# Fewer half swaps, larger loads of v and a two-part PSUM copy in the opening of a gated-attention and feed-forward kernel

## The chip, the cores and the metric

The kernel runs on one core of a Trainium2 chip. The metric is the device time of one execution in microseconds (us); the figure of a kernel is the median of its runs. The engines are PE (the matrix engine; its weight loads are shown apart as PEld), DVE (vector), ACT (scalar), POOL (GpSimd) and SP (which here only issues DMAs). POOL also issues DMAs, and an instruction that waits on POOL holds up everything behind it in POOL's queue.

## The reference

```python
# u, v: (8, 3072, 256)   z: (8, 3072, 64)   w1, w2: (256, 1024)   w_out: (1024, 256)
scores = (1.0 / S) * np.matmul(z, z.transpose(0, 2, 1))
attn = np.maximum(scores, 0.0) ** 2
x = (u * np.matmul(attn, v)).reshape(B * S, D)
out = np.maximum(x @ w1, x @ w2) @ w_out
```

Eight batches are independent of each other up to the last two lines, which work on all 24,576 rows alike.

## The kernel before, in words

**Tiling.** Each batch has 3,072 rows, cut into 24 tiles of 128. Four tiles make a group of 512 rows (six groups a batch), two groups make a couple (three couples a batch, 24 in all), and eight tiles of v, z or u are a "piece". A block `A[b, g, k]` is the squared, rectified score of query group `g` against key group `k`, kept in bf16. The scores are symmetric, so only the blocks with k >= g are computed (`score_pair`: two PE matmuls at L217 into PSUM, a Relu on ACT at L230 or on DVE at L228, a square on DVE at L238 or L236); the others are DMA transposes of them (`mirror`, L269, issued by SP).

**The feed-forward part** of a group (`ff`) multiplies with w1 - w2 (L447), rectifies on ACT (L454), and multiplies with w_out and the product of w2 and w_out (L470, L461); results leave by ACT copies (L482) and DMAs that POOL issues (L483). `second` runs it for both groups of the couple before, with DVE tasks of the next couple hooked between its steps.

**Attention, first batch.** The first four groups (`for i in range(PLAIN)`, L612) go one by one: the 128 keys of a tile are contracted in two halves of 64 rows that run side by side on PE, each half with its own two PSUM banks, matmuls at L285. During the first group z's transposes are made on PE (`zT_pe`, L122): PE turns n tiles into a PSUM tile, and one copy (L129) takes them to `zT`. It is called four times: tiles 0 to 3 and 4 to 11 are copied by DVE, tiles 12 to 19 and 20 to 23 by ACT.

**Attention, the plain couple.** Couple i = 2, groups 4 and 5 of the first batch, is the only one in `PLAIN_COUPLES`. Its four outputs D11, D12, D21, D22 (group, then half of the 256 columns of v) own one PSUM bank each. Every step issues two matmuls at L897: one contracts the upper 64 rows of a tile (half 0), the other the lower 64 rows (half 1), for two different outputs. For each "superblock" (1,024 keys; the order is 2, 1, 0) there are four runs of eight steps, so 32 steps, and 96 in all. `PLAIN_LANES` says which output each half works on in each run: half 0 takes D11, D12, D21, D22 and half 1 takes D21, D22, D11, D12.

**Bank swaps.** When an output moves from one half to the other, the first matmul of the new half must come after the last of the old one. `steps_of_couple` finds these places (`marks`, `waits`). One step after the marked matmul the kernel puts a no-op on POOL that waits for it (L878, `relays`), and the first matmul of the new half waits for that no-op. In POOL's queue the no-op stands in program order among the DMA issues.

**Loads of v.** `load_v` (L151) takes a piece or a part of it; `step = 2 if b else n` (L157) cuts it into DMAs of two tiles for every batch but the first. In the plain couple a plan issues v of batch 1 by six calls of four tiles, at steps 12, 20, 28, 36, 44 and 52, so twelve DMAs (L159). Every DMA that POOL issues gets one of eight semaphores in turn, and the built program lets an issue wait until the DMA eight issues before it has landed. DVE forms differences of v of batch 1 (`combine_v`, L173 to L176) in the feed-forward part after the plain couple.

**The other couples** (i >= 3) use seven products in place of eight and relay through ACT; nothing in them is edited.

## Time and profile before

| what | us |
|---|---|
| median of 6 runs | 911.57 |
| lowest and highest run | 909.49, 919.0 |
| the profiled execution, its own time | 911.91 |
| its span in the profile | 910.1 |
| PE busy | 898.8 (99%) |
| DVE, ACT, POOL busy | 723.0, 601.9, 163.8 |
| first group, up to the first drain | about 1 to 21 |
| plain couple, its matmuls | 80.06 to about 107.4 |
| v loads of batch 1 issued | 83.09 to 98.72 |
| DVE's differences of v of batch 1 | 114.14 to 119.3 |

The span is the stretch that the profile covers; 1.81 us of the execution lie outside it. A wait is listed with the engine and line that waited, an arrow, and what released it. "POOLq L878" is the no-op of a bank swap in POOL's queue. The engines' granted clock is full in every slice.

### The profile page before, as it was taken

What the parts mean: (1) busy time and instruction counts of PE and PEld (TensorE: products, weight loads), DVE (VectorE), ACT (ScalarE), POOL (GpSimd) and SP (SyncE); (2) the same over time, 40 slices, a digit from 0 to 9 for tenths busy, and PEclk for the clock granted to TensorE, in tenths of its full rate; (3) what the DMA queues carried; (4) which work ended last, traced back from release to release, by engine and by line L of the source; (5) the groups of instructions that cost most, each with busy time, mean ns of one, the idle gap of its engine ahead of it and who ended that gap; (6) DMA issues with size and microseconds to landing.
All of it is one profiled execution on the core that took longest, in us unless ns stands there. A gap on an engine that the chain in (4) does not pass through costs nothing.

```text
span 910.1 us, 19395 instructions
## 1 busy us (share of the span) xinstructions
PE 898.8 (99%) x7478; PEld 521.1 (57%) x7526; DVE 723.0 (79%) x1093; ACT 601.9 (66%) x1191; POOL 163.8 (18%) x309
## 2 busy tenths in 40 slices
PE   9999999999999999999999999999999999999998
PEld 4456455565565555665656656566465564655655
DVE  6773689879998799887997979979799788995640
ACT  7887866667676676667676666666766567673445
POOL 3103021212111121202113023030320212101000
PEclk9999999999999999999999999999999999999999
DMA  9999999999999996999989999899988999887201
GB/s 187 180 205 190 148 193 174 154 169 163 175 194 152 170 188 115 198 164 167 169 138 195 150 150 184 146 179 162 174 172 148 173 167 170 161 159 146 74 24 71
DMA packets 397421, 145.61 MB, mean 160 GB/s; under 512 B 362000, under 2 KB 389264, under 8 KB 397328
## 3 DMA queue, kind: packets, MB, share of 16 engines
q1 hardware_dynamic: 359040, 91.79, 65.3%
q0 software_dynamic: 38288, 52.58, 32.4%
q8 instruction: 59, 0.97, 0.5%
q14 instruction: 34, 0.28, 0.1%
HBM read 59.77 MB, written 25.17 MB: 93 GB/s over the span
## 4 chain that ended last, share of the span: by engine, by line
PE 95%; DMA 2%; DVE 1%; issue 1%; ACT 0%; POOL 0%; ACTq 0%; POOLq 0%
PE acc L897 44%; PE o_ps L470 18%; PE d_ps L447 18%; PE s_ps L217 7%; PE o_ps L461 5%; PE acc L285 3%; DMA v_sb<-in_v_dram 1%; DMA blk<-blk 1%; DVE blk L238 0%; PE acc L590 0%; ACT r_sb L230 0%; PE w2o_ps L679 0%; DVE w_sb L662 0%; ACT zT L129 0%; DVE blk L236 0%
## 5 line engine op out<-in xcount | busy, mean ns | idle before, releaser
L897 PE MATMUL acc<-blk,v_sb 64*128 64x512 bf16 x2208 | 451.0, 376 | 1.6 <-POOLq L878 1.6
L230 ACT ACTIVATE r_sb<-s_ps 128x512 bf16<-128x512 f32 (+3 forms) x672 | 335.9, 559 | 122.3 <-PE s_ps L217 79.9
L897 PE MATMUL acc<-blk,vt 64*128 64x512 bf16 x1512 | 364.4, 376 | 0.0
L897 PEld LDWEIGHTS <-v_sb 64*128 64x128 bf16 x2208 | 176.2, 94 | 135.0 <-issue 6.9
L238 DVE TENSOR_TENSOR blk<-r_sb 128x1024 bf16<-128x1024 bf16 x257 | 172.5, 689 | 89.6 <-ACT r_sb L230 89.0
L454 ACT ACTIVATE g_sb<-d_ps 128x512 bf16<-128x512 f32 x384 | 193.3, 630 | 28.6 <-PE acc L897 18.0
L470 PE MATMUL o_ps<-w_out_sb,g_sb 128*128 128x256 bf16 x1536 | 175.5, 273 | 0.0
L897 PEld LDWEIGHTS <-vt 64*128 64x128 bf16 x1512 | 139.2, 94 | 62.9
L447 PE MATMUL d_ps<-xT,w_sb 128*128 128x512 bf16 x720 | 167.7, 379 | 2.6 <-issue 0.2
L470 PEld LDWEIGHTS <-g_sb 128*128 128x128 bf16 x1536 | 150.3, 98 | 17.4
L482 ACT COPY o_sb<-o_ps 128x512 f32<-128x512 f32 (+1 forms) x98 | 56.3, 577 | 132.4 <-PE o_ps L470 132.4
L483 POOL DMA_DIRECT2D out_dram<-o_sb x88 | 48.1, 547 | 530.8 <-ACT o_sb L482 500.5
L774 DVE TENSOR_TENSOR h_sb<-h_sb,acc 128x512 f32<-128x512 f32 x168 | 109.4, 682 | 28.3 <-ACT h_sb L778 20.9
L217 PE MATMUL s_ps<-zT 64*128 64x512 bf16 (+3 forms) x676 | 126.3, 358 | 0.5 <-ACT zT L129 0.4
L447 PEld LDWEIGHTS <-w_sb 128*128 128x128 bf16 x768 | 73.3, 98 | 89.3 <-issue 9.7
L341 DVE TENSOR_TENSOR blk<-blk,blk 128x2048 bf16<-128x2048 bf16 x63 | 77.2, 1225 | 5.9 <-DMA blk<-blk 3.7
L337 DVE TENSOR_TENSOR blk<-blk,blk 128x2048 bf16<-128x2048 bf16 x63 | 76.8, 1219 | 0.0
L789 DVE TENSOR_TENSOR blk<-blk,blk 128x2048 bf16<-128x2048 bf16 x63 | 76.6, 1219 | 0.0
L345 DVE TENSOR_TENSOR blk<-blk,blk 128x2048 bf16<-128x2048 bf16 x63 | 73.3, 1219 | 1.8 <-DMA blk<-blk 1.7
L431 DVE SCALAR_TENSOR_TENSOR xT<-h_sb,uT 128x512 bf16<-128x512 f32 x96 | 62.0, 685 | 4.7 <-PE o_ps L461 4.7
L187 POOL DMA_DIRECT2D un<-in_u_dram x94 | 50.6, 564 | 80.0 <-DMA uT<-un 75.9
L236 DVE TENSOR_TENSOR blk<-r_sb 128x512 bf16<-128x512 bf16 (+3 forms) x162 | 46.5, 324 | 19.7 <-ACT r_sb L230 18.7
(48 smaller groups left out, 359.6 us busy)
## 6 DMA issues: line engine op xcount, KB each, us to landing
out_dram<-o_sb POOLq DMA_DIRECT2D x88, 256.0 KB, 3.6
un<-in_u_dram POOLq DMA_DIRECT2D x92, 128.0 KB, 5.4
v_sb<-in_v_dram POOLq DMA_DIRECT2D x86, 128.0 KB, 6.2
blk<-blk SPq DMA_TRANSPOSE x240, 4.9
zn<-in_z_dram POOLq DMA_DIRECT2D x21, 128.0 KB, 4.0
out_dram<-o_sb SPq DMA_DIRECT2D x6, 256.0 KB, 2.0
v_sb<-in_v_dram POOLq DMA_DIRECT2D x5, 256.0 KB, 7.7
blk<-in_moe_w_dram POOLq DMA_DIRECT2D x2, 512.0 KB, 7.1
```

The lines of the kernel that those rows point to most:

```text
L217: nc.tensor.matmul(s_ps[h][:, lo[h] :], zT[rows, z_at(b, blk * G + tiles[h]), :], zT[rows, q + lo[h] // P : q + G, :].rearrange("p t c -> ...
L230: nc.scalar.activation(o, s, AF.Relu)
L238: nc.vector.tensor_mul(a[:, k : k + 2, :], r, r)
L337: nc.vector.tensor_add(*alike(f["S1"], f["A21"], f["A22"]))
L341: nc.vector.tensor_sub(*alike(f["S2"], f["S1"], f["A11"]))
L345: nc.vector.tensor_sub(*alike(f["S3"], f["A11"], f["A21"]))
L447: nc.tensor.matmul(d_ps, w15_sb[:, kc, ts(nb, P)], xT[:, kc, :], start=(kc == 0), stop=(kc == KD - 1),)
L454: nc.scalar.activation(g_sb[:, nb, :], d_ps, AF.Relu)
L470: nc.tensor.matmul(o_ps[t // 2][:, t % 2, :], g_sb[:, nb, ts(t, P)], w_out_sb[:, nb, :], start=False, stop=(nb == KF - 1 and t % 2 == 1),)
L774: nc.vector.tensor_add(out, a, b_)
L789: nc.vector.tensor_sub(f["A12"].ap, f["A12"].ap, f["S2"].ap)
L897: mm = nc.tensor.matmul(a.out(acc[name]), w()[rows], a.moving(rows, j), start=name not in opened, stop=left[name] == 0,)
```

## The change

Three edits, none of which touches the arithmetic of a result other than the order of some additions.

- `zT_pe` copies its PSUM tile in parts of four tiles. The two calls with eight tiles (tiles 4 to 11 on DVE, 12 to 19 on ACT) now issue two copies each; the two calls with four tiles are as before.
- `load_v` takes the whole of what it is asked for in one DMA for batch 1 too, and the plan of the plain couple issues the six calls at steps 17, 25, 33, 41, 49 and 57. So six DMAs of four tiles stand where twelve of two tiles stood. Batches 2 and up keep two tiles a DMA.
- `plain_steps` reverses the lanes of every second superblock: in the second one half 0 takes D21, D22, D11, D12. An output then stays in its half from one superblock to the next, and only the swaps inside the superblocks are left: 12 in place of 20. No-ops stand after steps 7, 15, 39, 47, 71 and 79 (two each); before, they stood after every eighth step from 7 to 79.

```diff
         copy = nc.scalar.copy if engine == "act" else nc.vector.tensor_copy
-        copy(zT[:, lo : lo + n, :], tp)
+        for k in range(0, n, G):
+            copy(zT[:, lo + k : lo + k + G, :], tp[:, k : k + G, :])
...
-        step = 2 if b else n
+        step = 2 if b > 1 else n
...
-            for o in supers
-            for names in zip(*PLAIN_LANES)
+            for n, o in enumerate(supers)
+            for names in zip(*PLAIN_LANES[:: 1 - 2 * (n % 2)])
...
-                    *((12 + 8 * k, load_v, 1, k // 2, k % 2 * G, G) for k in range(6)),
+                    *((17 + 8 * k, load_v, 1, k // 2, k % 2 * G, G) for k in range(6)),
```

In the built program PE's instructions are the same in number and, but for the lanes, in order; DVE and ACT have one copy more each, POOL six DMA issues fewer. The first score matmul after a split copy waits for the copy's first part; a later one waits for the second.

## The prediction

> **What bounds the kernel now.** I read the page first, then who waited for whom on PE, then the timelines of the places where it waited.

> ```profile
> PE 898.8 (99%) x7478; PEld 521.1 (57%) x7526; DVE 723.0 (79%) x1093; ACT 601.9 (66%) x1191; POOL 163.8 (18%) x309
> ...
> DMA  9999999999999996999989999899988999887201
> ...
> L897 PE MATMUL acc<-blk,v_sb 64*128 64x512 bf16 x2208 | 451.0, 376 | 1.6 <-POOLq L878 1.6
> ```

> PE is busy for 898.8 of 910.1 us, so 11.3 us of idle time is all that reordering can win. The DMA engines are nearly full from start to end, but that costs only where PE waits for them. The third line is the one large group with idle time ahead of it: 1.6 us, ended by a no-op in POOL's queue (L878), a bank swap of the plain couple. The view of waits, PE alone (total, times, longest):

> ```profile
> PE acc L897 <- POOLq L878: 1.6, 1, 1.6
> ...
> PE s_ps L217 <- ACT zT L129: 0.4, 1, 0.4
> PE acc L285 <- DVE blk L238: 0.4, 1, 0.4
> PE acc L285 <- DMA blk<-blk: 0.3, 1, 0.3
> ```

> Two of these belong to what is edited: the swap, once, and the copy of z's turns by ACT, once. So 19 of 20 swaps cost PE nothing. By stretches, PE idles 0.78 us from 8 to 21, 0.93 to 43, 0.21 to 61, 0.11 to 80, 1.59 to 107 and 0.11 to 124: 3.73 us in all. From 124 to 852 it is 2.1 us of 728, so PE sets the pace there and a shift at 107 reaches the end undiminished.

> **The swap that stalls.** POOL's timeline in the plain couple (start, duration, idle time before and its releaser):

> ```profile
> 85.22 1.06 POOL L159 DMA_DIRECT2D v_sb<-in_v_dram  x2 [1.04 <-PE acc L897]
> ...
> 91.55 0.53 POOL L159 DMA_DIRECT2D v_sb<-in_v_dram  x1 [0.95 <-PE s_ps L217]
> 94.17 0.53 POOL L159 DMA_DIRECT2D v_sb<-in_v_dram  x1 [2.10 <-DMA v_sb<-in_v_dram]
> 96.04 0.53 POOL L159 DMA_DIRECT2D v_sb<-in_v_dram  x1 [1.34 <-DMA v_sb<-in_v_dram]
> 98.72 0.53 POOL L159 DMA_DIRECT2D v_sb<-in_v_dram  x1 [2.15 <-DMA v_sb<-in_v_dram]
> ```

> The last three issues wait for earlier v loads to land. They are the 10th to 12th of twelve, and each waits for the issue eight before it: the 12th for the 4th, issued at 85.75 (second of the pair at 85.22), which lands at 98.7, 13 us later. The no-op of the next swap stands behind it. PE at that time:

> ```profile
> 96.47 0.81 PE L897 MATMUL acc<-blk,v_sb 64*128 64x512 bf16 x6
> 98.87 0.60 PE L897 MATMUL acc<-blk,v_sb 64*128 64x512 bf16 x4 [1.59 <-POOLq L878]
> ```

> PE stops at 97.28 and resumes at 98.87. A step takes (27.33 - 1.59) / 96 = 0.268 us, so 97.28 is step (97.28 - 80.06) / 0.268 = 64, the border between the second superblock and the third.

> **The change part by part.**

> *Reversed lanes.* The swaps at steps 32, 40, 64 and 72 (two outputs' worth at each border) disappear, and with them the stalled one. Eight no-ops of 17 ns are nothing on POOL, which is 18% busy. Kept are the no-ops issued at steps 8, 16, 40, 48, 72 and 80, needed eight steps (2.1 us) later. The matmuls are as many as before, at the same places, and read the same blocks in the same steps, so no transposed block is needed sooner.

> *Six loads.* The loads at steps 17, 25, 33, 41, 49 and 57 start at about 80.06 + 0.268 s: 84.6, 86.8, 88.9, 91.0, 93.2 and 95.3. Eight issues back of each are the output DMAs at 71.47 and 73.22 and the four u loads from 73.76 to 75.4. Each lies 13 us or more before the load that waits for it, and the page gives 3.6 and 5.4 us as the median landing of the two kinds. So no load waits for a landing, and no no-op is held: those of step 40 precede their load, those of 48 stand behind one issue of 0.53 us, and those of 72 and 80 come 15 steps and more after the last load. Either edit alone should free step 64; together they save the 1.6 us once, not twice. POOL's six issues less (6 x 0.53 = 3.2 us) are hidden: POOL is idle there most of the time, and without that cover they would be a gain.

> *Landing.* DVE reads v of batch 1 only later:

> ```profile
> 114.14 0.42 DVE L173 TENSOR_TENSOR vt<-v_sb 128x512 bf16<-128x512 bf16 x1
> ...
> 117.58 0.42 DVE L173 TENSOR_TENSOR vt<-v_sb 128x512 bf16<-128x512 bf16 x1
> ```

> The third piece (last two loads) is read at 117.58, or 115.6 after a gain of 2 us: 20.3 us after its last issue at 95.3. DMA in the plain couple (count, KB each, median us to landing):

> ```profile
> v_sb<-in_v_dram POOLq DMA_DIRECT2D x12, 128.0 KB, 10.9
> ...
> blk<-blk SPq DMA_TRANSPOSE x2, 14.6
> ```

> A load of twice the bytes may take from 10.9 (if the queue of transposes sets it) to twice that, 21.8 (if its own bytes do). I take 13, near the first, because the bytes are as many as before and are asked for over a shorter time; then it lands at 108, with 7 us to spare. The transposes of this stage (longest landing 19.1 us, done by 108.4) are first read from 110.5 on.

> [...] I count nothing beyond the stall. [...]

> *The two-part copy.* The opening (several engines, one answer):

> ```profile
> 6.81 5.04 ACT L230 ACTIVATE r_sb<-s_ps 128x512 bf16<-128x512 f32 x9 [0.91 <-PE s_ps L217]
> 6.82 0.68 DVE L129 COPY zT<-tpz 128x1024 bf16<-128x1024 bf16 x1
> ...
> 11.38 1.04 PE L285 MATMUL acc<-blk,v_sb 64*128 64x512 bf16 x8
> 11.74 1.02 ACT L129 COPY zT<-tpz 128x1024 bf16<-128x1024 bf16 x1
> 12.81 0.39 PE L217 MATMUL s_ps<-zT 64*128 64x512 bf16 x2 [0.39 <-ACT zT L129]
> 13.24 0.60 ACT L230 ACTIVATE r_sb<-s_ps 128x512 bf16<-128x512 f32 x1 [0.48 <-PE s_ps L217]
> ```

> On ACT the first part takes 0.59 us (the four-tile copy at 16.36), so it ends at 11.74 + 0.59 = 12.33, and PE, free at 12.42, need not wait: 0.39 less. The second part ends near 12.9 instead of 12.76; the next ACT instruction waits for PE until 13.24, 12.87 after the shift, so at most some 0.03 comes back. I take 0.37. On DVE the first part (0.42) ends at 7.24 instead of 7.50, so the score at 7.55 can start about 0.26 sooner; but ACT works without a break from 6.81 to 11.8 on nine activations and then the copy, and it is the copy that PE awaits, so nothing is gained. DVE's extra 0.16 falls before an instruction that waits for ACT at 7.93.

> [...] Whether the 0.37 survives is less sure: at 20.93 and 37.9 PE waits again for DVE (0.4) and for a transpose (0.3). Their releasers follow PE's earlier work, so they should shift too, but with full DMA engines a landing may not. Bounds: 0 (nothing carried; the loss of 0.16 is hidden) to 0.39.

> *Sum*, on the profiled execution: 911.91 - 1.6 - 0.37 = 909.94 (span 908.1). It stands 0.34 above the median, so against the median 911.57 - 1.97 = 909.6.

> **Rivals.**

> 1. The opening's shift is swallowed by the waits at 20.9 or 37.9; only the swap is won: 911.57 - 1.6 = 910.0. For it: those waits exist, and DMA is full there. Against: they are released by work that follows PE.
> 2. The change does not do what it says: POOL is held by something else and PE stops at a kept swap (56, 80 or 88) for as long: 911.6. For it: loads still stand between swaps. Against: all eight-back landings are over.
> 3. More than the sum: fewer DMAs relieve the opening's and the plain couple's other waits. The cap is all of PE's idle time from 8 to 124, 3.73: 907.8.
> 4. Slower: the last load lands late behind SP's transposes and DVE's differences start late. DVE's last sum for the next couple ends at 127.48 and is wanted near 128.7 (step 20 of it), 1.2 us of slack. So a landing of more than 20.3 + 1.2 = 21.5 us costs PE one for one, and from 23.5 on the kernel is slower than before. At 26 us it is 911.57 - 1.97 + 4.5 = 914.1. For it: 19.1 us was seen in that stage for a transpose. Against: the loads' longest was 13.

> **How the numbers follow.** Chances: forecast 0.55, rivals in order 0.22, 0.05, 0.12, 0.06. The time is the forecast's, 909.6. The six runs spread from 909.49 to 911.91 with two above, so about 1 us of noise stands on each case: the forecast's own range is 908.5 to 911, and with rival 3 below and rivals 1 and 2 above 907.3 to 912.2. Over 1% (9.1 us), about what a measurement can tell from no change, lies beyond the cap of 3.73 for a gain (0.02, if the median's high runs fall away or appear) and needs a landing above 32 us for a loss (0.03). So 0.95 within 1%.

> **What the profile after would show.** Right: no wait of L897 for L878; no load L159 waiting for a v landing, all six issued by 96; no wait of L217 for L129; the plain couple 25.7 us long; a span near 908.1. Wrong: a wait for L878 at another step (rival 2), L173 waiting for a v landing and idle time of L897 after 123 (rival 4), or the waits at 20.9 and 37.9 grown by 0.4 (rival 1).

## The result and the profile after

| | median, us | lowest to highest |
|---|---|---|
| before, same chip | 916.23 (69 runs) | 909.44 to 924.45 |
| after | 915.0 (32 runs) | 909.48 to 924.17 |

The ratio is 0.9991 [0.9972, 1.0011]: no change that a measurement can tell. The forecast of "within 1%" holds. The time does not: 915.0 lies above the range of 907.3 to 912.2, and so does the kernel before, whose 69 runs have a median 4.7 us above that of the six that the forecast started from. Every ratio in this document leaves out the runs that are over 1.5% longer than the fastest of their kernel; below, this matters for e7, where 12 of 22 runs are left out, so that there the median tells more.

The profiled execution after took 913.1 us (span 911.3, mean granted clock 0.998). Its page, beside the first fence of the prediction (busy time, then groups by line; L897 is now L898, L217 is L218):

```profile
PE 898.8 (99%) x7478; PEld 519.9 (57%) x7526; DVE 724.4 (79%) x1094; ACT 602.0 (66%) x1192; POOL 160.9 (18%) x303
...
L898 PE MATMUL acc<-blk,v_sb 64*128 64x512 bf16 x2208 | 451.8, 378 | 0.0
...
L218 PE MATMUL s_ps<-zT 64*128 64x512 bf16 (+3 forms) x676 | 126.0, 358 | 2.2 <-DMA zT<-zd 2.0
```

The large group has lost its 1.6 us of idle time, as forecast. Another group has got 2.0 us: a score matmul that waited for a transpose of z. The view of waits, PE alone:

```profile
PE s_ps L218 <- DMA zT<-zd: 2.0, 1, 2.0
PE acc L286 <- DVE blk L239: 1.8, 2, 1.4
```

The wait for POOL's no-op and the wait for ACT's copy are gone from the list; the one for DVE's square has grown from 0.4 to 1.8. What the edits did can be seen in the timelines. POOL's loads of v:

```profile
85.02 1.62 POOL L160 DMA_DIRECT2D v_sb<-in_v_dram  x3 [3.61 <-PE acc L898]
95.47 0.53 POOL L160 DMA_DIRECT2D v_sb<-in_v_dram  x1 [8.84 <-PE s_ps L218]
97.33 1.06 POOL L160 DMA_DIRECT2D v_sb<-in_v_dram  x2 [1.33 <-PE s_ps L218]
```

All six wait for PE, none for a landing. They did not start at the times of their steps, though (forecast 84.6 to 95.3): three went out together from 85.02 on, and the other three at 95.47, 97.33 and 97.86, after a stop of PE that comes below. And the opening, ACT first, then PE:

```profile
12.41 1.08 ACT L130 COPY zT<-tpz 128x512 bf16<-128x512 bf16 x2
13.48 0.60 ACT L231 ACTIVATE r_sb<-s_ps 128x512 bf16<-128x512 f32 x1
```

```profile
11.91 1.04 PE L286 MATMUL acc<-blk,v_sb 64*128 64x512 bf16 x8
13.06 0.39 PE L218 MATMUL s_ps<-zT 64*128 64x512 bf16 x2
```

Two copies take 1.08 us (forecast 2 x 0.59 = 1.18) where one took 1.02, and PE's score starts 0.11 us after the matmuls ahead of it (11.91 + 1.04 = 12.95), not 0.39.

**Where the time went.** The n-th PE instruction of both traces can be laid side by side (7,478 in each). After minus before, in us, by the time in before: +0.67 at 10 (DVE's square of the opening held PE for 1.39 near 8 us; before that PE had been 0.64 ahead), +0.25 at 14 (0.42 won back, 0.27 of it at the copy), -0.22 at 39 (the wait for a mirror at 37.6 has fallen away), -0.23 at 86.5; then **+3.63** at 91; +1.87 at 99 (the no-op's wait is missing: -1.76); and +1.19 at the end (small differences over 800 us, -0.68). So between these two executions the forecast gains are there (1.76 and 0.27 for 1.6 and 0.37), and one new stop took 3.86 us. PE there:

```profile
86.32 0.81 PE L898 MATMUL acc<-blk,v_sb 64*128 64x512 bf16 x6
89.13 0.39 PE L218 MATMUL s_ps<-zT 64*128 64x512 bf16 x2 [2.00 <-DMA zT<-zd]
```

and by stretches of 1 us (length; busy time of PE, PEld, DVE, ACT and POOL; granted clock; DMA share, which counts a packet's whole time where it starts and so can pass 1; GB/s):

```profile
90.00:91.00 1.00, 1.00 (x8) 0.45 (x6) 0.33 (x1) 0.63 (x2) 0.00 (x0) 0.50 1.13 206
91.00:92.00 1.00, 1.00 (x8) 0.33 (x6) 0.36 (x1) 0.90 (x2) 0.00 (x0) 0.50 1.11 192
92.00:93.00 1.00, 1.00 (x8) 0.32 (x5) 0.69 (x1) 0.18 (x1) 0.00 (x0) 0.50 1.14 208
93.00:94.00 1.00, 1.00 (x10) 0.44 (x8) 0.00 (x0) 0.39 (x1) 0.00 (x0) 0.80 2.55 128
```

After the stop PE ran at half clock for 3.41 us (89.98 to 93.39). Of the 3.86, 2.00 are waiting and 1.70 slow matmuls (half of 3.41; the ledger grows from 1.93 to 3.63 over it), which "busy" does not tell from fast ones. The other 0.16 I put down to the overlap of neighbouring matmuls, which a stop breaks (at full clock a pair of scores is shown 0.38 long, the next matmul starting 0.22 after it began: 104.42 and 104.64 in after); likewise the no-op's wait of 1.59 is 1.76 in the ledger. The last section has what the traces show of the stops that half clock followed.

The wait is for z's second batch, which SP turns by DMA transposes. SP's queue in the kernel before, and after:

```profile
57.92 18.43 SPq L269 DMA_TRANSPOSE blk<-blk  x6
76.45 6.66 SPq L143 DMA_TRANSPOSE zT<-zd  x2
```

```profile
59.67 19.44 SPq L270 DMA_TRANSPOSE blk<-blk  x6
79.20 6.35 SPq L144 DMA_TRANSPOSE zT<-zd  x2
```

Before, PE's first use of a turn, and the time from issue to landing of the two turns:

```profile
87.19 0.38 PE L217 MATMUL s_ps<-zT 64*128 64x512 bf16 x2
DMA to landing us min/median/max: 9.8/10.2/10.6
```

The turns stand behind six mirrors and are issued one after another almost without a gap (76.35 to 76.45 in before, 79.11 to 79.20 in after). In the kernel before the first was issued at 76.45 and landed at 86.28, 0.9 us before PE used it at 87.19; after, it was issued at 79.20 and landed at 89.08. They took 9.8 and 9.9 us: after, it was late because it was issued late, and that because the mirrors ahead of it began 1.75 us later and took 1.0 longer. The slack was 0.9 us, which the forecast left out.

### The profile page after: what moved, and what is told of

Read it like the earlier page. It is cut to its first block, busy times and chain, and to the rows that moved or that the text cites. A ratio compares the mean times of both kernels' runs of the same rounds, so it can differ in the third digit from the quotient of the medians.

```text
span 911.3 us, 19380 instructions
## 1 busy us (share of the span) xinstructions
PE 898.8 (99%) x7478; PEld 519.9 (57%) x7526; DVE 724.4 (79%) x1094; ACT 602.0 (66%) x1192; POOL 160.9 (18%) x303
## 4 chain that ended last, share of the span: by engine, by line
PE 96%; DVE 1%; DMA 1%; issue 1%; ACT 1%; ACTq 0%; DVEq 0%
PE acc L898 44%; PE o_ps L471 18%; PE d_ps L448 18%; PE s_ps L218 7%; PE o_ps L462 5%; PE acc L286 3%; DMA zT<-zd 1%; DVE blk L239 1%; ACT r_sb L231 1%; PE acc L591 0%; PE w2o_ps L680 0%; DVE xT L432 0%; PE tpz L125 0%; DVE w_sb L663 0%; DVE h_sb L311 0%
## 5 line engine op out<-in xcount | busy, mean ns | idle before, releaser
L898 PE MATMUL acc<-blk,v_sb 64*128 64x512 bf16 x2208 | 451.8, 378 | 0.0
L898 PE MATMUL acc<-blk,vt 64*128 64x512 bf16 x1512 | 364.1, 376 | 0.0
L898 PEld LDWEIGHTS <-v_sb 64*128 64x128 bf16 x2208 | 176.6, 94 | 135.4 <-issue 7.8
L898 PEld LDWEIGHTS <-vt 64*128 64x128 bf16 x1512 | 139.2, 94 | 62.2
L775 DVE TENSOR_TENSOR h_sb<-h_sb,acc 128x512 f32<-128x512 f32 x168 | 109.5, 682 | 28.3 <-ACT h_sb L779 20.9
L218 PE MATMUL s_ps<-zT 64*128 64x512 bf16 (+3 forms) x676 | 126.0, 358 | 2.2 <-DMA zT<-zd 2.0
L188 POOL DMA_DIRECT2D un<-in_u_dram x94 | 50.8, 563 | 76.4 <-DMA uT<-un 71.2
L237 DVE TENSOR_TENSOR blk<-r_sb 128x512 bf16<-128x512 bf16 (+3 forms) x162 | 46.3, 323 | 19.9 <-ACT r_sb L231 18.9
## 6 DMA issues: line engine op xcount, KB each, us to landing
un<-in_u_dram POOLq DMA_DIRECT2D x92, 128.0 KB, 5.1
v_sb<-in_v_dram POOLq DMA_DIRECT2D x74, 128.0 KB, 5.4
zn<-in_z_dram POOLq DMA_DIRECT2D x21, 128.0 KB, 4.1
```

The source lines that it names most:

```text
L218: nc.tensor.matmul(s_ps[h][:, lo[h] :], zT[rows, z_at(b, blk * G + tiles[h]), :], zT[rows, q + lo[h] // P : q + G, :].rearrange("p t c -> ...
L775: nc.vector.tensor_add(out, a, b_)
L898: mm = nc.tensor.matmul(a.out(acc[name]), w()[rows], a.moving(rows, j), start=name not in opened, stop=left[name] == 0,)
```

## The experiments

All kernels compute the whole reference. The time of each (median, number of runs, ratio to the kernel before on the same chip with its interval), and PE's stops of 0.9 us or more after the opening, in its one profile:

| kernel | median (n) | ratio | stops of PE: at, us, for what | mean clock |
|---|---|---|---|---|
| e1 before | 915.89 (22) | 0.9981 [0.9954, 1.0008] | none | 0.999 |
| e2 lanes alone | 918.21 (14) | 1.0015 [0.9978, 1.0053] | 87.5, 8.23, z's turn | 0.996 |
| e3 loads alone | 915.01 (22) | 0.9984 [0.9957, 1.001] | 87.4, 3.06, z's turn | 0.998 |
| e4 copy alone | 915.09 (22) | 0.9976 [0.9948, 1.0003] | 36.8, 2.96, mirror | 0.998 |
| e5 after, z sooner | 915.84 (14) | 0.9986 [0.9955, 1.0017] | 37.2, 3.24, mirror; 180.1, 1.65, z's turn | 0.998 |
| e6 before, z sooner | 918.37 (22) | 0.9993 [0.9964, 1.0023] | 90.6, 8.57, mirror | 0.996 |
| e7 e5, w_out later | 925.66 (22) | 1.0025 [0.9986, 1.0064] | 37.4, 2.54, mirror; 92.0, 9.26, mirror | 0.994 |
| e8 after, u later | 914.72 (14) | 0.9998 [0.9959, 1.0036] | 37.5, 1.16, mirror; 123.7, 3.31, DVE sum | 0.998 |
| e9 e8, v later | 916.15 (14) | 0.9992 [0.9955, 1.0029] | 121.6, 3.21, DVE vt; 126.1, 5.02, DVE sum | 0.994 |
| e10 e9, weights later | 923.54 (14) | 1.0066 [1.0029, 1.0104] | 48.9, 1.07, mirror; 51.2, 2.47, mirror; 128.0, 5.02, DVE sum | 0.993 |
| e11 before, u and weights later | 921.38 (17) | 1.0054 [1.0025, 1.0083] | 49.5, 1.26, mirror; 52.1, 2.43, mirror; 100.3, 3.80, POOL's no-op | 0.994 |
| e12 after, w1 and w2 later | 917.82 (22) | 1.0021 [0.9993, 1.0049] | 37.4, 2.75, mirror; 164.2, 2.33, DVE; 178.8, 1.48, DVE | 0.997 |
| e13 before, w1 and w2 sooner | 915.06 (14) | 0.9982 [0.9945, 1.002] | 37.6, 0.99, mirror; 98.2, 0.95, POOL's no-op; 175.7, 5.92, DVE | 0.996 |
| e14 lanes and loads, no copy | 915.62 (22) | 0.9987 [0.9958, 1.0016] | 136.9, 3.28, DVE | 1.000 |
| e15 e12, z before two mirrors | 917.45 (22) | 1.0014 [0.9988, 1.0041] | 37.8, 2.48, mirror | 0.998 |
| e16 after again | 917.66 (20) | 1.003 [1.0003, 1.0057] | 86.9, 10.56, z's turn | 0.994 |
| e17 after, third | 916.91 (12) | 0.9999 [0.997, 1.0028] | 37.2, 2.71, mirror | 0.998 |
| e18 before, third | 917.73 (20) | 1.0027 [1.0001, 1.0053] | 87.1, 5.79, z's turn | 0.996 |

Where the table names DVE, DVE itself had waited for a landing: for u's turns in e8 to e10 (6.2, 11.3 and 8.4 us), for mirrors in e12 to e14 (up to 5.1, 6.6 and 4.6).

### The parts alone (e1 to e4)

e1 is the kernel before. e2 takes only the reversed lanes, e3 only the six loads with their steps, e4 only the copy in parts.

> The kernel before, unchanged, to see how far one kernel spreads. Theory J (landings of DMAs differ by some us from run to run, and PE stops wherever one is late, which then also costs it some 3.4 us at half clock): the runs spread over 909 to 921 as the kernel after does, runs at a mean clock of 1.000 take 909 to 912, and each 0.002 below 1 goes with 2 to 4 us more. Theory N (the spread of the kernel after comes from a wait that the change brought in): nearly all runs of this one are at clock 1.000, and they take 909 to 913.

> Only the reversed lanes. The wait of the second superblock's end on POOL's no-op (1.6 us) is gone on both theories, since that swap no longer exists. Theory J: ratio to before 0.997 to 1.000, the same spread of clocks as before; z's turns for batch 1 make PE wait in some executions and not in others. Theory N with the lanes at fault: a wait of PE for z's turns or for a no-op of a kept swap in the profile, and more time than before.

> Only the six later, larger loads of v for batch 1, with all 20 swaps. Both theories: no load waits for the landing of an earlier load, so no swap is held and PE does not wait for POOL. Theory J: ratio 0.997 to 1.000. Theory N with the loads at fault: PE waits for z's turns or DVE for v, 2 us or more, and the ratio is 1.001 or more.

> Only the two-part copy of z's PE turns. Theory J: PE's wait for ACT's copy in the opening falls from 0.4 to about 0, the wait for POOL's no-op stays 0 to some us by luck, ratio 0.998 to 1.001. Theory N with the split at fault: DVE's first square next to POOL's casts takes over 2 us as in the profile after (2.27 against 0.80), PE stops 1.4 us near 8 us, and the opening ends at least 0.2 us later than before's.

The kernel before, unchanged, shows in a second execution no wait for POOL's no-op at all (its waits of PE, the largest first):

```profile
PE acc L285 <- DVE blk L238: 1.2, 2, 0.8
PE acc L590 <- DVE blk L565: 1.2, 1, 1.2
PE s_ps L217 <- ACT zT L129: 0.5, 1, 0.5
```

The 1.6 us that the change removes is there in some executions and not in others: of seven profiles with neither reversed lanes nor later loads, three have it (before 1.59, e13 0.95, e11 3.80) and four do not (e1, e4, e6, e18). Lanes alone and loads alone, as the forecast said of them, each show no such wait (e2, e3), but one profile each cannot prove it; both show the wait for z's turns. The copy alone wins at 13 us and ends the first group at 20.17, the earliest of all, and then PE stops:

```profile
39.79 1.46 PE L286 MATMUL acc<-blk,v_sb 64*128 64x512 bf16 x6 [2.96 <-DMA blk<-blk]
```

This is the place of rival 1, with ten times its 0.3 us: what was gained at 13 us is lost at 37, and half clock follows from 39.83.

### z's turns sooner (e5 to e7)

```diff
-                if (i, n) in ((2, 8), (3, 10)):
-                    turn_z(1, i - 2)
-                if (i, n) == (3, 14):
+                if (i, n) in ((2, 8), (3, 3), (3, 10)):
+                    turn_z(1, (i - 2) + n // 10)
+                if (i, n) == (3, 1):
...
-            [lambda: turn_z(1, 2)]
+            [lambda: None]
```

e5 is this edit on the changed kernel, e6 the same on the kernel before, e7 is e5 with `(1, 10)` made `(2, 2)` where w_out is loaded.

> The kernel after, with z's turns for pieces 1 and 2 of batch 1 put two and three transposes earlier in SP's queue (their load four tiles' steps earlier). Theory J (the wait for z's turns in the plain couple, 0 to 8 us by luck, and the 3.4 us at half clock behind it make most of the spread): no wait of PE for zT in the profile, over half of the runs at clock 0.999 or more against a tenth to a fifth before, median 909 to 912, ratio to before 0.992 to 0.996. Theory M (the spread has many places, this is one of them): the median falls by less than 2 us and the clocks keep their spread.

> The kernel before, with the same earlier turns of z. Its difference to e5 is the change alone, with this wait out of the way. Theory J with the sum of the prediction: 1 to 2 us above e5, with PE waiting for POOL's no-op in the profile. Theory Z (the change is worth nothing, because the no-op's wait is itself luck): within 0.7 us of e5.

> e5, and w_out loaded in the third group in place of the second, so that it doesn't land together with the first transposed blocks. Theory J: PE's wait for a transposed block near 37 us (0.3 in the profile before, 3.0 with half clock behind it in the one with the split alone) is gone, the rest of the low-clock runs go with it, median 908 to 910, up to 2 us below e5. Theory M: no difference to e5 beyond 0.7 us.

z's turns come in time at 87 in all three, and no kernel is faster; e7 is slower, its median 8.5 us above that of before on the same chip (917.16). In e6 and e7 the mirror that now stands behind them is late at 90 to 92, by 8.6 and 9.3 us. SP issued the transposes of this stage almost without a gap (no more than 0.2 us between two, from 55.91 to 108.18 us of before); to put one forward put another back.

### POOL's loads later (e8 to e11)

```diff
-            + [lambda g=g: load_u(0, g) for g in (4, 5)],
+            + [lambda: None] * 2,
...
-                    (1, turn_u, 0, 4),
-                    (4, turn_u, 0, 5),
-                    *((17 + 8 * k, load_v, 1, k // 2, k % 2 * G, G) for k in range(6)),
+                    (6, load_u, 0, 4),
+                    (10, load_u, 0, 5),
+                    (44, turn_u, 0, 4),
+                    (48, turn_u, 0, 5),
+                    *((33 + 8 * k, load_v, 1, k // 2, k % 2 * G, G) for k in range(6)),
```

e8 has the edit of u only, e9 that of v too. e10 also loads w1 and w2 at step 12 of the second group and w_out at step 2 of the third (`((1, 12), (2, 2))`), so that the mirror needed at 37 is under way first. e11 has u and weights of e10 on the kernel before.

> The kernel after, with the u loads of groups 4 and 5 issued at steps 6 and 10 of the plain couple and turned at steps 44 and 48 (before: loaded from 73.5 us on and turned at steps 1 and 4). z's turns and all mirrors keep their places. Theory K (a transpose of SP takes about 2 us alone and 6 to 10 us while POOL's loads are in flight, and the u loads are what delays z's turns and the mirrors): z's turns land by 83, PE doesn't wait for them, and half of the runs or more have a clock of 0.999 or more; median 909.5 to 912.5. Theory L (the output DMAs and v's loads do it just as well, or SP's own backlog): z's turns land at 85 or later as before, and the spread stays.

> e8, with the six loads of v at steps 33 to 73 in place of 17 to 57. Theory K: as e8, and up to 1 us less where v's loads would hold up the last mirror needed in the second superblock. Theory L with v at fault: only this one, not e8, loses the wait for z's turns. If v comes too late, DVE waits for it near 117 (no more than 2 us) and PE near 128.

> e9, with the weights w1 and w2 loaded at the 12th tile of the second group (before: 20th of the first) and w_out at the 2nd of the third (before: 10th of the second). Theory K: the mirror that PE needs near 37 us lands by 34, PE's wait for it (0.3 to 3.2 us in five profiles, two of them with half clock behind) is gone, nearly all runs have a clock of 0.999 or more, median 908 to 910.5. Theory L: the wait only moves to a later mirror, and the clocks keep their spread.

> The kernel before with the same late u loads and late weights, and its own lanes, twelve loads of v from step 12 and one-part copies. Theory K and the sum of the prediction: little spread, and the change's own worth shows as 1 to 2.5 us above e8 to e10, with PE waiting for POOL's no-op or for ACT's copy. Theory Z (the edits are worth nothing once the transposes are on time): within 0.7 us of e10.

z's turns landed at 84.5 in e8 and 82.5 in e9: without u's loads beside them they come in time. From issue to landing the first turn took 4.0 to 5.2 us in e8 to e11, and 8.2 to 18.9 in the twelve profiles that have it and u's loads in their old places. In e10 the mirror needed at 37 landed at 32.8, issued at 27.3, where those of the table's waits at 37 landed at 38.6 to 40.4. So POOL's loads in flight delayed the transposes in these profiles. But each of these loads has to fly at some time, and then what needs it is late. The waits of e8, PE and then DVE, and those of e10:

```profile
PE acc L900 <- DVE blk L342: 3.3, 1, 3.3
...
DVE xT L432 <- DMA uT<-un: 6.2, 1, 6.2
```

```profile
PE acc L900 <- DVE blk L342: 5.0, 1, 5.0
PE acc L286 <- DMA blk<-blk: 3.5, 2, 2.5
...
DVE xT L432 <- DMA uT<-un: 8.4, 1, 8.4
```

PE waits for DVE's sums for the next couple, and DVE had stood still for u's turn, which the edit itself put behind a mirror (in e8 issued at 109.37, landed at 114.48); from there to the end of PE's stop DVE worked without a break. So the stops of e8 to e10 after 120 are the price of moving u, and say nothing of other transfers. The two stops of e10 and e11 near 50 are mirrors with the moved weights beside them (in e10 weights issued from 31.1 on, the mirror at 33.9, landed at 49.9). e8 is no better by its median; its four runs at a mean clock of 1.000 average 909.4, the least of all kernels, but four are few. e10 and e11 are slower than before, by 0.7 and 0.5%, beyond their intervals. e11 brought the no-op's wait back, at 3.80.

### The order of the weights at 37 us (e12, e13, e15) and the copy left out (e14)

In e4, e5, e7 and e8 POOL issued the weights from 0.4 us before to 0.3 after SP issued u's second turn, and this turn landed at 27.9 to 34.9; in the other kernels up to here the weights came 0.9 us or more after it, and it landed at 23.6 to 24.5. e12 moves w1 and w2 from `(0, 20)` to `(1, 0)` on the changed kernel, e13 to `(0, 17)` on the kernel before. e15 is e12 with the mirrors of one block behind z's turns. e14 is the changed kernel with the one-part copy.

> The kernel after with w1 and w2 loaded at the start of the second group in place of the 20th tile of the first, some 1.5 to 2 us later. Theory W (the two-part copy ends the first group earlier, the weights then overtake u's second turn, and that turn and the mirror behind it land late): the second turn lands by 25, PE's wait near 37 us is under 0.5, and with the first group ending at 20.2 to 21.2 the waits up to 60 us sum to less than 2. Theory V (the mirror near 37 us is late by luck, whatever the weights do): a wait of 1 us or more there in spite of it.

> The kernel before, one-part copies, with w1 and w2 loaded at the 17th tile of the first group, some 0.9 to 1.3 us earlier than now. Theory W: u's second turn lands at 28 or later, and PE waits 1 to 4 us for the mirror near 37 us, as the kernels with the two-part copy do; the median is 1 us or more above before. Theory V: the wait stays at 0 to 0.3 us.

> The change without the two-part copy: reversed lanes and six loads alone. Theory W: PE waits about 0.4 us for ACT's copy near 12.5, the first group ends at 20.9 to 21.6, and the wait near 37 is 0 to 0.3; no wait for POOL's no-op; the median is no higher than that of after. Theory V: no difference near 37 us to the kernels with the split copy.

> e12, and the two mirrors of block 5 against groups 0 and 1 (first read at step 64 of the plain couple) put behind z's turns in SP's queue, where they stood ahead of them. Theory W with SP's order as the cause of the second wait: z's turns land by 80, PE's waits from 80 to 130 us are under 1 us, most runs have a clock of 0.999 or more, and the median is 908.5 to 911, below before and after. Theory V: another transpose is late in their place, and the median is within 0.3% of before.

e13 delayed u's second turn to 33.5, as the theory of the weights said, and PE waited 0.99 us at 37. e12 and e15 had the turn on time (24.9, 24.8), and the mirror was as late as ever (40.1, 40.2): waits of 2.75 and 2.48. So weights close behind it did delay the turn (later, e16 and e17 fit: 27.4 and 34.3, with waits of 0.3 and 2.71), but the turn alone does not explain the wait at 37; what decides there stays open. e15 put z's turns right (landed 76.0) and kept the wait at 37. e14 stops neither at 37, as expected of a one-part copy, nor at 87 (z's turn landed at 85.8), and stops at 137 instead.

### The same kernels again (e16 to e18)

> The changed kernel once more, nothing edited. Theory L (the stops are set by when DMAs land, and that differs from execution to execution of one and the same kernel): the first profile's stop of 2.00 us at 87 for z's turns is not a property of the kernel. Here it is another size (0 to 8 us), or absent, and the execution's time is about 911 plus 1.8 us for each 0.001 that the mean clock lies under 1.000, as in the runs of the kernel before. No wait for POOL's no-op in the plain couple and at most 0.11 us behind ACT's copy near 13. If the first group ends before 21.0 us, PE waits 1 to 3.5 us for a mirror at 37. Theory K (the lanes and loads themselves make z's turns late): a stop of 1.5 us or more for z's turns at 87 again, landing 88 to 96.

> The changed kernel a third time, nothing edited. Theory L: as for the second, and the three profiles of this one kernel differ among themselves in where PE stops; their spans differ by 1 us or more. Theory K: all three stop at 87 for z's turns.

> The kernel before once more, nothing edited. Theory L: the wait for POOL's no-op near 98 was 1.59 us in the first profile and 0 in the second; here it may be either, and runs at a mean clock of 0.999 or 1.000 have a mean of 911 to 912, the same as such runs of the changed kernel within 0.7 us. Theory N (the no-op wait is a fixed cost of the kernel before): 1.4 to 1.8 us again, and undisturbed runs of the changed kernel are 1.5 us or more below those of this one.

PE's longest wait in e16, in e17 and in e18:

```profile
PE s_ps L218 <- DMA zT<-zd: 10.6, 1, 10.6
```

```profile
PE acc L286 <- DMA blk<-blk: 2.7, 1, 2.7
```

```profile
PE s_ps L217 <- DMA zT<-zd: 5.8, 1, 5.8
```

Three executions of the changed kernel waited 2.0, 10.6 and 0 us at 87, and 0, 0.3 and 2.7 at 37. Three of the kernel before waited 0, 0 and 5.8 at 87, and for the no-op 1.6, 0 and 0. So the stops belong to the execution, and an unedited kernel has them too. They also depend on each other: in e17 z's turn landed at 88.34, later than PE's usual 87.2, and PE did not wait only because its stop at 37 had made it 3.5 us later. The first part of the theory of landings holds. The theory that lanes and loads make z's turns late falls: e18 stops without them, e14 has both and no stop there, and the first of the two edits acts at step 12, at 83 us, when the first turn has been issued (76.4 to 80.0 in the kernels that have it in its old place). A fixed no-op wait falls too (e1, e18). e16 and e18 read 0.3% slower than before, e18 being the kernel before itself: a ratio of 1.003 with an interval just off 1 is no evidence here.

What a late transpose looks like is seen in the DMA view from 60 to 107 us, of the kernel before and of e16 (queue: packets, MB, share; then count and median us to landing):

```profile
q1 hardware_dynamic: 19375, 4.87, 74.9%
...
zT<-zd SPq DMA_TRANSPOSE x2, 10.2
```

```profile
q1 hardware_dynamic: 16417, 4.13, 86.5%
...
zT<-zd SPq DMA_TRANSPOSE x2, 20.8
```

The transposes' queue moved fewer packets in more of the engines' time: each was slower. What made them so in this execution, no view shows; the loads were slow as well. Issued 0.65 us sooner than in the first profile of the changed kernel (78.55), z's turn landed 8.3 us later (97.42), with three loads of v beside it that took 19.7 to 21.5 us (5.9 to 9.4 in that first profile).

**All runs by their clock.** Each run comes with its mean granted clock, and one stretch of 3.4 us at half clock takes 0.5 x 3.4 / 911 = 0.0019 off it. The runs of both kernels, share and mean time (all runs that have a clock on record):

| mean clock | before, 320 runs | after, 65 runs |
|---|---|---|
| 0.999 or more (no such stretch) | 31%, 911.4 | 8%, 911.4 |
| 0.997 to 0.998 (one) | 18%, 915.4 | 38%, 914.9 |
| 0.995 to 0.996 (two, or longer) | 35%, 918.9 | 35%, 916.8 |
| 0.994 or less | 16%, 921.7 | 18%, 922.1 |
| all, mean | 916.39 | 916.61 |

A run without such a stretch takes 911.4 us with either kernel, though only five runs of the changed one are such. Each step of the clock costs 2 to 5 us, some 3.5 on average, its stop included. The changed kernel has fewer runs without one, but this share also differs between sets of runs of the unedited kernel: on the chip of e18 it is 19 of 47 for before and 2 of 20 for e18. The table's waits at 37 point to a reason: of eight profiles with one-part copies (the kernel before thrice, e2, e3, e6, e13, e14) only e13, whose weights come sooner, stopped there for 0.9 us or more; of eight with copies in parts and w1 and w2 where they were (after thrice, e4, e5, e7, e8, e9) five did, for 1.2 to 3.2. That is no proof that it costs on average, since the means are equal within their scatter. Nor do the clocks settle it: the change without the two-part copy (e14) has 9 of 22 runs without a stretch at half clock, but the copy alone (e4) 5 of 22, beside 6 of 22 for e1.

## Why the prediction was right and wrong

- **The no-op's wait goes: right.** None of 13 profiles with reversed lanes or later loads shows it, against three of seven without; that either edit alone suffices rests on e2 and e3, one profile each. The step in the ledger is -1.76, forecast -1.6. The reading of its cause holds but for a detail: the fourth load landed at 98.43, not at 98.7.
- **It is worth 1.6 us of every run: wrong.** It was read from one execution and carried to the median. It is absent in two of three profiles of the kernel before. Runs without a stretch at half clock are equal for the two kernels, 911.4, where the forecast would have the changed one 2.0 lower.
- **The copy: right in its place, wrong in what is left of it.** PE's wait behind it was 0.11 where 0.39 was forecast to fall to 0 (the others with a copy in parts: 0 to 0.11; with one: 0.39 to 0.54), the copy in two parts cost ACT 0.06 more than one (1.08 against 1.02) where the bounds count a loss of 0.16, and the first group ends 0.5 us sooner on average (20.7 against 21.2). "Their releasers follow PE's earlier work, so they should shift too" failed at 37 in five of eight such profiles: the mirror does not come sooner, and PE waits there for longer. Rival 1 was the truer case, and too mild.
- **"The transposes of this stage ... are first read from 110.5 on": wrong.** z's turns are of this stage and are read from 87.19 on. Their slack was 0.9 us. The slower rival sought a late landing with a price per us, the right kind, but at v, which was in time (no wait of DVE for v in after).
- **"About 1 us of noise stands on each case": wrong**, and this is the step that put the time outside the range. The six runs already had 917.17 and 919.0 among them, and these two, set aside as the exceptions, were nearer to the median of 69 runs (916.23) than the other four. The noise is a stop of 1 to 10 us for a landing, in most profiles with some 1.7 us lost at half clock behind it. A range that took these two as cases, less the 1.97 of the sum, would have reached to 917.
- **The signs**: no wait for L878 and none for a landing of v, as forecast. Missed are "all six issued by 96" (the last at 97.86), the plain couple's 25.7 us (29.4; 25.6 without the 3.86 of the stop) and the span of 908.1 (911.3); of the wait for the copy 0.11 is left.
- **Within 1%: right**, since no wait that is edited is above 0.2% of the time.
- **Loads of 256 KB against SP's transposes**: whether they slow them more than loads of 128 KB was not separated. The packets did grow (POOL's queue from 83 to 107 us: 1,846 for 2.06 MB before, 1,085 for 2.15 MB after). z's turns were late with loads of 128 KB (e2, e18) and of 256 KB (after, e3, e16), and in time with both (e1, e14).

## What to carry to other kernels

A wait in one profile is one execution's wait. Before it is counted as a gain, follow it back past the engine that it names: the no-op's wait stood under POOL and PE's waits for DVE after 120 us under DVE, but both began with a DMA landing. A wait that begins so did not repeat here (0 to 3.80 us for the no-op); the wait behind ACT's copy did (0.39 to 0.54 in nine profiles with a one-part copy). For the first kind, ask of all transfers in flight there how much slack each has, and take a second profile. With the DMA engines nearly full (busy for nine tenths or more in 29 of the 40 slices of before), each reordering tried here (e5 to e13, e15) left a stop elsewhere. Whether fewer bytes would remove the stops was not tried.

## What the runs showed of the hardware

```profile
86.57:89.98 3.41, 1.41 (x14) 0.47 (x12) 1.15 (x2) 1.24 (x3) 0.07 (x1) 1.00 1.14 181
89.98:93.39 3.41, 3.41 (x18) 1.24 (x16) 1.38 (x2) 1.74 (x4) 0.00 (x0) 0.50 1.12 204
```

```profile
135.24:138.66 3.42, 1.61 (x16) 0.61 (x13) 1.01 (x2) 0.22 (x1) 0.00 (x0) 1.00 1.28 165
138.66:142.07 3.41, 1.72 (x15) 0.81 (x16) 3.41 (x5) 0.86 (x2) 0.00 (x0) 1.00 1.02 206
142.07:145.48 3.41, 3.41 (x34) 1.73 (x32) 3.31 (x8) 2.98 (x7) 1.49 (x3) 1.00 0.75 129
```

- A DMA transpose landed 2.27 us after its issue at the shortest (mirrors, 800.66 in before), 3.1 to 3.3 with little beside it (u's turns issued at 19.85 and 21.21 in after, with 16 packets of POOL's queue until 24.33), and 8.2 to 18.9 with POOL's loads in flight (z's first turn: 9.9 in after, with 550 packets of that queue from 79.20 to 89.08; 18.9 in e16).
- DVE's square in the opening took 2.27 us from 7.19 in after and 0.80 from 7.93 in before, with POOL's casts beside it in both (7.15 to 9.72, 6.68 to 9.33). It held PE for 0 to 1.39 us from one profile to the next, among one-part kernels too (0 to 0.83).
